# Attention and two feed-forward blocks on one core: w3 kept in DRAM as float32, and low parts of weights and of g made by VectorE

## Chip, core and metric

One core of a Trainium2 chip runs the whole program in one launch. The metric is device time in microseconds (us) of one execution; lower is better.

## What is computed

```python
# q, k, v: (4, 8, 576, 64), s: (4, 8, 576)
scores = q @ k.T / sqrt(64);  cum = cumsum(max(s, 0))
scores = where(causal, -1e9, scores + min(cum_k - cum_q, 0))
x = softmax(scores) @ v            # 32 heads, joined to (2304 tokens, 512)
h = x @ w_in                       # (512, 2048)
x = (h - tanh(h)) @ w_out          # g = h - tanh(h); (2048, 512)
y = ((x @ w1) * (x @ w2)) @ w3 @ w_out2    # (512, 1024) twice, (1024, 1024), (1024, 512)
```

The weights arrive as 64-bit floats, q, k, v and s as float32. The result must have float32 precision.

## The kernel before

**Precision.** TensorE multiplies in a rounded float32 format (`F32R`). An operand is therefore held as two tiles, a high part (the value rounded by a copy) and a low part (value minus high part), and a product is three matmuls: high x high, high x low, low x high (`mm3`, L113). `split` (L63) makes the two parts: the high part with a copy on ScalarE, the low part with a subtraction on GpSimd, unless the caller passes other engines as `hi` and `lo`. `plain` (L84) turns 64-bit weights into float32 with three integer operations on VectorE into a tile `cvt`; `convert` (L97) is `plain` followed by `split`.

**Stage 1, to about 430 us: attention and the first half of the first feed-forward block.** The 32 heads go in 16 pairs, each pair in two parts, along a list of numbered steps (L501 to L640): scores on TensorE, minimum and maximum on VectorE (L247), exponentials on ScalarE (L273), transposes and products with v on TensorE. Bias tiles come from GpSimd (L206, L218) and ScalarE (L208), out of a tile `cb` that a DMA spreads from DRAM. In between, `ffn` (L400) runs hidden chunks 0 to 7 of the 16 chunks of `w_in` and `w_out`, for nine blocks of 256 tokens: `h`, then tanh on ScalarE, `th = h - tanh(h)` on VectorE (L463), then g's high part `gh` and low part `gl` (L464 to L467), then `y` (L431). For blocks 0 and 1 `gh` is a ScalarE copy and `gl` a GpSimd subtraction; from block 2 both are VectorE's. `conversions` (L369) converts the 16 weight tiles of chunks 0 to 7; `parked` (L383) converts the 16 of chunks 8 to 15 and stores both parts to `wf_d` (`park`, L103), to be fetched when the first ones are free. Both use `split`'s GpSimd subtraction.

**Stage 2, about 430 to 622 us: chunks 8 to 15** for five blocks of up to 512 tokens (`ffn_rest`, L704). One step of `preparations` (L656) runs per chunk: it reads w1 and w2, forms sums for a seven-product matrix scheme and stores their two parts in `wg_d`; converts `w_out2` into the tiles `wo2`; and converts w3 in 8 pieces of two halves (L676 to L688). Pieces 6 and 7 stay in SBUF (`kept`), the others go to `w3_d` as two parts, 1,024 KB each.

**Stage 3, about 622 to 672 us: the product of w3 and w_out2** (`w3o`, L835 to L850), in eight groups of 24 matmuls in the order 6, 7, 4, 5, 0, 1, 2, 3. `fetch_w3` (L828) loads a piece from `w3_d` into one of two buffers `w3b`; the first two are the kept ones, so the load of a piece waits until the group two places earlier has been multiplied. ScalarE copies each result out (L844); `operands` (L759) and `weights` (L807) prepare the next stage on ScalarE and VectorE.

**Stage 4, to the end:** both products of x with w1 and w2, their elementwise product, and the product with the folded weights (L861 to L941), with weight tiles S and A loaded from `wg_d` (L787, L789).

**What sets the order.** TensorE's order is the order in which the program is written. For the other engines and for SP, whose queue issues the DMAs, a scheduler with a timeline of its own sets the order when the program is built; after that each engine works strictly in its order. Buffers are counted by pool tag: two of `raw` and two of `cvt` in pool `cv`, two of `park` in `wt`, one of `park` in `f2`, three each of `gh` and `gl`.

Of the kernel before, what the change touches and what calls it, by code (L numbers as in the profile page):

```python
# [37 lines left out]
def tile_kernel(ctx: ExitStack, tc: tile.TileContext, qk, v, s, w_in, w_out, w1, w2, w3t, w_o2, outT):  # L38
# [13 lines left out]

    cum_d = dr.tile([NH, S], F32, tag="cum_d", name="cum_d")
    yp_d = dr.tile([P, NC, NT], F32, tag="yp_d", name="yp_d")
    w3_d = dr.tile([NG, P, 2, 2, DM], F32, tag="w3_d", name="w3_d")
    wf_d = dr.tile([2 * (NF - F1), P, 2, DM], F32, tag="wf_d", name="wf_d")
    wg_d = dr.tile([NG, P, 7, 2, 2 * P], F32, tag="wg_d", name="wg_d")
    wo_d = dr.tile([7, 2, P, 2, 2, 2 * P], F32, tag="wo_d", name="wo_d")
# [4 lines left out]
    def split(dst_hi, dst_lo, src, hi=None, lo=None):  # L63
        i = (hi or nc.scalar.copy)(dst_hi, src)  # L64
        (lo or nc.gpsimd.tensor_sub)(dst_lo, src, dst_hi.bitcast(F32))  # L65
        return i
# [17 lines left out]
    def plain(raw, name, behind=None):  # L84

        r3 = raw.rearrange("p (f two) -> p f two", two=2)
        t = cv.tile([P, DM], U32, tag="cvt", name=f"cvt_{name}")
        i = nc.vector.tensor_scalar(out=t, in0=r3[:, :, 1], scalar1=3, scalar2=0x3FFFFFFF,
                                    op0=ALU.logical_shift_left, op1=ALU.bitwise_and)
        in_turn(i, behind)  # L90
        nc.vector.scalar_tensor_tensor(out=t, in0=r3[:, :, 0], scalar=29, in1=t,
                                       op0=ALU.logical_shift_right, op1=ALU.bitwise_or)
        nc.vector.scalar_tensor_tensor(out=t, in0=r3[:, :, 1], scalar=0xC0000000, in1=t,
                                       op0=ALU.bitwise_and, op1=ALU.bitwise_or)
        return t.bitcast(F32)

    def convert(raw, name, w=None, lo=None, behind=None):  # L97
        t = plain(raw, name, behind)
        w = slot(name) if w is None else w
        split(w[:, 0, :], w[:, 1, :], t, lo=lo)  # L100
        return w

    def park(raw, name, dst, pool, behind):  # L103

        w = convert(raw, name, pool.tile([P, 2, DM], F32R, tag="park", name=f"park_{name}", bufs=1), behind=behind)
        nc.sync.dma_start(dst, w.bitcast(F32))

    def fetch(name, src):
# [14 lines left out]
    with ExitStack() as actx:  # L123
# [245 lines left out]
        def conversions(fs):  # L369
            todo = [(d, f, src[f], f"{n}{f}") for f in fs for d, src, n in ((win, w_in, "win"), (wout, w_out, "wout"))]  # L370
            raws = []
            for m in range(2):
                raws.append(load_raw(*todo[m][2:], behind=latest[0]))
                yield
            for m, (d, f, src, n) in enumerate(todo):
                d[f] = convert(raws.pop(0), n, behind=least[0])
                if m + 2 < len(todo):
                    raws.append(load_raw(*todo[m + 2][2:], behind=latest[0]))
                yield
# [20 lines left out]
        def ffn():  # L400
            pend = []
            cut = {}

            def ready(blk):
                return blk < NB and all(written[b] >= min(S, (blk + 1) * BLK - S * b) for b in range(B))

            def cut_x(blk, lo):
                xs = cut.setdefault(blk, [])
                c, c0 = len(xs), blk * BLK
                x = f2.tile([P, 2, BLK], F32R, tag="xhl", name=f"xhl{blk}_{c}", bufs=6)  # L410
                split(x[:, 0, :], x[:, 1, :], xy[:, c, c0:c0 + BLK], lo=lo)
                xs.append(x)

            for blk in range(NB):
                c0 = blk * BLK
                while not ready(blk):
                    yield False
                while len(cut.get(blk, ())) < NC:
                    cut_x(blk, nc.vector.tensor_sub)
                xs = cut[blk]  # L420
                ys = []

                def add_y(f, gh, gl, end, ys=ys, blk=blk):
                    while f not in wout:
                        next(conv)
                    if f == 0:
                        ys.extend(ps_y.tile([P, 2, BLK], F32, tag=f"y{z}", name=f"y{z}_{blk}") for z in range(2))
                    for n, (z, x) in enumerate(((0, gh), (1, gh), (0, gl))):
                        for c in range(NC):
                            o = ys[c // 2][:, c % 2, :]  # L430
                            nc.tensor.matmul(o, wout[f][:, z, P * c:P * c + P], x,  # L431
                                             start=f == 0 and n == 0 and c % 2 == 0, stop=f == F1 - 1 and n == 2,
                                             skip_group_check=True)
                            if n == 1 and c == 1:
                                yield True
                    if f == F1 - 1:
                        after[1].append(end)

                def end_y(ys=ys, blk=blk, c0=c0):
                    for z in range(2):  # L440
                        yo = f2.tile([P, 2, BLK], F32R, tag="xhl", name=f"yo{z}_{blk}", bufs=6).bitcast(F32)
                        nc.scalar.copy(yo, ys[z])
                        nc.sync.dma_start(yp_d[:, 2 * z:2 * z + 2, c0:c0 + BLK], yo)

                for f in range(F1):
                    while f not in win:
                        next(conv)
                    late = written[B - 1] == S
                    ph = ps_a.tile([P, 512], F32, tag="s", name=f"h{blk}_{f}") if late else ps_h.tile([P, 512], F32, tag="h", name=f"h{blk}_{f}")
                    hh = ph[:, :BLK]  # L450
                    for c in range(NC):
                        pace[0] = mm3(hh, win[f], P * c, xs[c][:, 0, :], xs[c][:, 1, :], c == 0, c == NC - 1)
                        if c == 1:
                            yield True
                    t = f2.tile([P, BLK], F32, tag="th", name=f"th{blk}_{f}")
                    gh = f2.tile([P, BLK], F32R, tag="gh", name=f"gh{blk}_{f}", bufs=3)
                    gl = f2.tile([P, BLK], F32R, tag="gl", name=f"gl{blk}_{f}", bufs=3)

                    def tanh(t=t, hh=hh):
                        nc.scalar.activation(t, hh, AF.Tanh)  # L460

                    def rest(t=t, hh=hh, gh=gh, gl=gl, blk=blk):
                        nc.vector.tensor_sub(t, hh, t)  # L463
                        if blk < 2:  # L464
                            split(gh, gl, t)
                        else:
                            split(gh, gl, t, hi=nc.vector.tensor_copy, lo=nc.vector.tensor_sub)  # L467

                    after[0].append(tanh)
                    after[1].append(rest)  # L470
                    yield True
                    if len(pend) > late:
                        yield from pend.pop(0)
                    pend.append(add_y(f, gh, gl, end_y))
                    if f >= 3 and ready(blk + 1) and len(cut.get(blk + 1, ())) < NC:
                        cut_x(blk + 1, nc.vector.tensor_sub)
                    if blk == NB - 1 and f:
                        next(conv2, None)
                        next(conv2, None)
                    yield True  # L480
            for p in pend:
                yield from p
            yield True
            yield True
# [166 lines left out]
    def load_w3(f, z):  # L651
        return load_raw(w3t[f, :, 4 * z:4 * z + 4].rearrange("p m c -> p (m c)"), f"w3_{f}_{z}", behind=pace[0])
# [3 lines left out]
    def preparations():  # L656
# [19 lines left out]
        for f in range(NG):  # L676
            if f == NG // 2:
                for m in range(NG):
                    convert(load_raw(w_o2[m], f"wo2_{m}", behind=pace[0]), f"wo2_{m}", wo2[m], lo=nc.vector.tensor_sub)
                    yield  # L680
            pk = wt.tile([P, 2, 2, DM], F32R, tag="park", name=f"w3p{f}", bufs=2)
            for z in range(2):
                convert(load_w3(f, z), f"w3_{f}_{z}", pk[:, z], lo=nc.vector.tensor_sub)
                yield
            if f in W3ORDER[:2]:
                kept[f] = pk
            else:
                nc.sync.dma_start(w3_d[f], pk.bitcast(F32))  # L688

    with ExitStack() as bctx:  # L690
        b2 = bctx.enter_context(tc.tile_pool(name="b2", bufs=2, reuse_waits="tile"))
# [135 lines left out]

    def fetch_w3(f):  # L828
        if f not in w3b:
            w3b[f] = wt.tile([P, 2, 2, DM], F32R, tag="park", name=f"w3b{f}", bufs=2)  # L830
            nc.sync.dma_start(w3b[f].bitcast(F32), w3_d[f])
        return w3b[f]

    ctx.enter_context(tc.manual_schedule(engines={mybir.EngineType.PE}))
# [221 lines left out]
```

## Time and profile before

| what | value |
|---|---|
| median of 3 runs | 943.5 us (942.43 to 948.34) |
| the profiled execution: time, span | 942.7 us, 940.9 us |
| TensorE busy | 914.4 us, 97% of the span |
| VectorE, ScalarE, GpSimd busy | 641.4, 452.6, 211.7 us |
| mean granted TensorE clock | 0.995 |
| HBM read, written | 151.86 MB, 46.29 MB |

The span is the time from the first to the last instruction; 1.8 us of the execution lie around it. TensorE's busy time is modelled from pipelined matmuls, so gaps in it are the surer reading. Each engine works through its queue in order, so an instruction that waits holds up all that stand behind it.

### The profile page before, as it was taken

How to read it: one execution, taken by the hardware profiler on the slowest of the kernel's cores; microseconds unless marked ns; L12 is line 12 of the kernel's file. 1: busy time of each engine (PE TensorE's matmuls, PEld its weight loads, DVE VectorE, ACT ScalarE, POOL GpSimd, SP SyncE). 2: the span in 40 equal slices, each digit the busy share in tenths (PEclk: the TensorE clock that was granted, in tenths of full speed). 3: DMA queues.
4: the chain of work that ended last, by engine and by line, in shares of the span. 5: the costliest groups of instructions: out<-in, count | busy, mean ns of one | idle time of the engine just before them, and what ended most of it. 6: DMA issues, size and time to landing. Idle time of an engine off the chain costs nothing.

```text
span 940.9 us, 16373 instructions
## 1 busy us (share of the span) xinstructions
PE 914.4 (97%) x6022; PEld 800.3 (85%) x6025; DVE 641.4 (68%) x1403; ACT 452.6 (48%) x1061; POOL 211.7 (22%) x210
## 2 busy tenths in 40 slices
PE   8889999899999999999999999998999999999998
PEld 4567777788888889998888888987899999999998
DVE  7677777787777866776999978763145747564555
ACT  4567887777776753323434433342123432433133
POOL 2245856666555410000000000000011111111100
PEclk9799999999999999999999999999999999999999
DMA  5655365535454423489687736258399877777774
GB/s 161 196 164 170 114 205 182 168 137 179 154 169 147 152 98 100 169 308 405 250 293 279 265 110 209 85 207 291 119 319 325 322 257 271 262 271 258 284 267 148
DMA packets 59072, 199.21 MB, mean 212 GB/s; under 512 B 6544, under 2 KB 21040, under 8 KB 53360
## 3 DMA queue, kind: packets, MB, share of 16 engines
q1 hardware_dynamic: 58992, 198.17, 60.8%
q8 instruction: 47, 0.77, 0.3%
q14 instruction: 33, 0.27, 0.1%
HBM read 151.86 MB, written 46.29 MB: 211 GB/s over the span
## 4 chain that ended last, share of the span: by engine, by line
PE 81%; DMA 7%; DVE 5%; ACT 3%; issue 2%; POOL 1%; SPq 1%; ACTq 0%; DVEq 0%; POOLq 0%
PE hb L117 10%; PE yb L117 10%; PE h L117 9%; PE W L861 9%; PE y L431 9%; PE oW L924 5%; PE Y L861 5%; PE s_B L229 4%; PE pv L327 4%; PE oY L924 4%; PE pt_B L301 3%; PE w3o L117 2%; DMA w3b<-w_d 2%; PE V L861 2%; DMA cb<-cum_d 2%
## 5 line engine op out<-in xcount | busy, mean ns | idle before, releaser
L117 PE MATMUL h<-xhl,win 128*128 128x256 f32 x864 | 120.6, 286 | 2.8 <-DVE xhl L65 1.9
L117 PEld LDWEIGHTS h<-xhl,win 128*128 128x128 f32 x864 | 105.8, 188 | 13.4 <-issue 4.3
L994 POOL TENSOR_TENSOR xy<-c,c 128x384 f32<-128x384 f32 x12 | 15.4, 1280 | 425.4 <-DVE c L983 425.4
L117 PE MATMUL hb<-x,win 128*128 128x512 f32 (+1 forms) x480 | 104.9, 367 | 0.0
L117 PEld LDWEIGHTS hb<-x,win 128*128 128x128 f32 x480 | 83.9, 188 | 15.0
L206 POOL TENSOR_SCALAR pr<-cb,cq 128x384 f32<-128x384 f32 (+1 forms) x48 | 90.8, 1904 | 22.8 <-DMA cb<-cum_d 14.3
L117 PE MATMUL yb<-ghb,wout 128*128 128x512 f32 (+1 forms) x320 | 95.6, 367 | 0.0
L431 PE MATMUL y<-gh,wout 128*128 128x256 f32 x576 | 85.2, 287 | 0.5 <-DVE gh L64 0.5
L290 ACT ACTIVATE pr<-pr,nm 128x128 f32<-128x128 f32 (+2 forms) x120 | 71.5, 598 | 19.0 <-DVE nm L268 18.9
L431 PEld LDWEIGHTS y<-gh,wout 128*128 128x128 f32 x576 | 72.5, 189 | 3.7 <-issue 2.0
L117 PEld LDWEIGHTS yb<-ghb,wout 128*128 128x128 f32 x320 | 58.2, 188 | 9.9
L117 PE MATMUL yb<-glb,wout 128*128 128x512 f32 (+1 forms) x160 | 58.4, 367 | 0.0
L301 PE MATMUL pt_B<-ident,pr 96*128 96x96 f32 (+1 forms) x384 | 51.4, 256 | 1.4 <-DVE cq L601 0.9
L268 DVE CUSTOM_DVE_ANT_0 pr<-s_B,pr 96x512 f32<-96x512 f32 (+1 forms) x72 | 44.1, 638 | 8.7 <-PE s_B L229 8.7
L431 PE MATMUL y<-gl,wout 128*128 128x256 f32 x288 | 45.1, 279 | 3.2 <-POOL gl L65 2.7
L301 PEld LDWEIGHTS pt_B<-ident,pr 96*128 96x128 f32 (+1 forms) x384 | 41.2, 143 | 5.7 <-issue 3.3
L463 DVE TENSOR_TENSOR th<-h,th 128x256 f32<-128x256 f32 x72 | 30.0, 417 | 22.3 <-ACT th L460 21.6
L310 ACT COPY pf_B<-pt_B 128x512 f32<-128x512 f32 (+2 forms) x72 | 35.8, 499 | 19.3 <-PE pt_B L301 19.3
L460 ACT ACTIVATE th<-h 128x256 f32<-128x256 f32 x72 | 26.8, 373 | 34.4 <-PE h L117 34.3
L872 ACT COPY s<-Y 128x384 f32<-128x384 f32 x24 | 11.6, 482 | 63.0 <-PE Y L861 60.5
L431 PEld LDWEIGHTS y<-gl,wout 128*128 128x128 f32 x288 | 38.3, 188 | 3.8 <-POOL gl L65 3.1
L64 ACT CAST ghb<-thb 128x512 fp32r<-128x512 f32 (+1 forms) x40 | 23.2, 579 | 35.2 <-DVE thb L725 34.5
(215 smaller groups left out, 2076.7 us busy)
## 6 DMA issues: line engine op xcount, KB each, us to landing
S<-wg_d SPq DMA_DIRECT2D x24, 1024.0 KB
wo<-wo_d SPq DMA_DIRECT2D x42, 512.0 KB
A<-wg_d SPq DMA_DIRECT2D x24, 768.0 KB
qk<-in_qk SPq DMA_DIRECT2D x16, 576.0 KB
raw_win<-in_w_in SPq DMA_DIRECT2D x16, 512.0 KB
raw_wout<-in_w_out SPq DMA_DIRECT2D x16, 512.0 KB
raw_w<-in_w SPq DMA_DIRECT2D x16, 512.0 KB
wg_d<-pks SPq DMA_DIRECT2D x8, 1024.0 KB
```

The source lines that it names most:

```text
L117: i = nc.tensor.matmul(ps, a, b, start=first and n == 0, stop=last and n == 2, skip_group_check=skip)
L206: nc.gpsimd.tensor_scalar(out=t[:pw, e, :w], in0=p.cb[:pw, e, :w], scalar1=c, scalar2=0.0, op0=ALU.add, op1=ALU.min)
L229: latest[0] = nc.tensor.matmul(ps[e][:PW[i], o:o + k1 - k0], w[r, 0, CH0[i]:CH0[i] + PW[i]], x[r, 1, k0:k1], start=z == 0 and (not p.first ...
L268: least[0] = nc.vector.tensor_tensor_reduce(out=t[:pw, k0:k1], in0=ps[:pw, o:o + k1 - k0], in1=t[:pw, k0:k1], scale=-0.125, scalar=nm[:pw, ...
L290: last_exp[0] = nc.scalar.activation(t[:pw, :], t[:pw, :], AF.Exp, bias=m, scale=-1.0, accum_out=p.sums[:pw, e, c:c + 1])
L301: nc.tensor.transpose(pt[:, at:at + pw], p.pr[i][:pw, e, KC0[kj]:KC0[kj] + P], ident[:pw, :pw])
L310: (nc.vector.tensor_copy if j == "B2" and not p.first else nc.scalar.copy)(pf[:, :at], pt[:, :at])
L327: nc.tensor.matmul(p.pv[D * e:D * e + D, c:p.nq], p.vs[:, e, kj], pf[:, beg:end], start=z == 0, stop=z == len(todo) - 1, skip_group_check= ...
L431: nc.tensor.matmul(o, wout[f][:, z, P * c:P * c + P], x, start=f == 0 and n == 0 and c % 2 == 0, stop=f == F1 - 1 and n == 2, skip_group_c ...
L463: nc.vector.tensor_sub(t, hh, t)
L861: i = nc.tensor.matmul(ps[:, :T], w[:, x, P * j:P * j + P], b[:, y, j], start=first and j == n == 0, stop=stop and j == 1 and n == 2, skip ...
L924: nc.tensor.matmul(ps[:, :T], w[:, a, q % 2, P * j:P * j + P], x[:, b, q], start=o in ("B11", "B21", "T1") and q == z == 0, stop=o in ("T4 ...
```

## The change

There are four edits. (1) w3: pieces 0 to 5 are stored in `w3_d` as plain float32, one half at a time straight from the `cvt` tile, 256 KB per store instead of one store of 1,024 KB per piece; `fetch_w3` loads 512 KB into a `raw` buffer and makes the two parts there, the high part on ScalarE, the low part on VectorE. (2) `conversions`: the low part of the 16 weight tiles by VectorE instead of GpSimd. (3) `park`: the same for the 16 parked tiles. (4) block 1 of the first half of the feed-forward block: both parts of g by VectorE.

```diff
-    w3_d = dr.tile([NG, P, 2, 2, DM], F32, tag="w3_d", name="w3_d")
+    w3_d = dr.tile([NG, P, 2, DM], F32, tag="w3_d", name="w3_d")
...
     def park(raw, name, dst, pool, behind):
-        w = convert(raw, name, pool.tile([P, 2, DM], F32R, tag="park", name=f"park_{name}", bufs=1), behind=behind)
+        w = convert(raw, name, pool.tile([P, 2, DM], F32R, tag="park", name=f"park_{name}", bufs=1), lo=nc.vector.tensor_sub, behind=behind)
...
-                d[f] = convert(raws.pop(0), n, behind=least[0])
+                d[f] = convert(raws.pop(0), n, lo=nc.vector.tensor_sub, behind=least[0])
...
-                        if blk < 2:
+                        if blk < 1:
                             split(gh, gl, t)
                         else:
                             split(gh, gl, t, hi=nc.vector.tensor_copy, lo=nc.vector.tensor_sub)
...
-            pk = wt.tile([P, 2, 2, DM], F32R, tag="park", name=f"w3p{f}", bufs=2)
+            if f in W3ORDER[:2]:
+                kept[f] = wt.tile([P, 2, 2, DM], F32R, tag="park", name=f"w3p{f}", bufs=2)
             for z in range(2):
-                convert(load_w3(f, z), f"w3_{f}_{z}", pk[:, z], lo=nc.vector.tensor_sub)
+                if f in kept:
+                    convert(load_w3(f, z), f"w3_{f}_{z}", kept[f][:, z], lo=nc.vector.tensor_sub)
+                else:
+                    nc.sync.dma_start(w3_d[f, :, z], plain(load_w3(f, z), f"w3_{f}_{z}"))
                 yield
-            if f in W3ORDER[:2]:
-                kept[f] = pk
-            else:
-                nc.sync.dma_start(w3_d[f], pk.bitcast(F32))
...
     def fetch_w3(f):
         if f not in w3b:
+            raw = cv.tile([P, 2 * DM], U32, tag="raw", name=f"raw_w3b{f}").bitcast(F32).rearrange("p (z c) -> p z c", z=2)
+            nc.sync.dma_start(raw, w3_d[f])
             w3b[f] = wt.tile([P, 2, 2, DM], F32R, tag="park", name=f"w3b{f}", bufs=2)
-            nc.sync.dma_start(w3b[f].bitcast(F32), w3_d[f])
+            split(w3b[f][:, :, 0], w3b[f][:, :, 1], raw, lo=nc.vector.tensor_sub)
         return w3b[f]
```

TensorE's order stays as it was. The first place is SP's queue between stages 2 and 3, before the change (S and A are stage 4's weight tiles, w3b a piece of w3, yp the stored partial y):

```order
L709 DMA yp2048_7774<-yp_d_74 128x4x256
L787 DMA S_0_8166<-wg_d_77 128x2048
L789 DMA A_0_8168<-wg_d_77 128x1536
L787 DMA S_1_8243<-wg_d_77 128x2048
L789 DMA A_1_8245<-wg_d_77 128x1536
L831 DMA w3b4_8133<-w3_d_75 128x2048
L831 DMA w3b5_8164<-w3_d_75 128x2048
L831 DMA w3b0_8201<-w3_d_75 128x2048
```

And the same place after it:

```order
L831 DMA raw_w3b4_8109<-w3_d_75 128x1024
L709 DMA yp2048_7750<-yp_d_74 128x4x256
L831 DMA raw_w3b5_8143<-w3_d_75 128x1024
L787 DMA S_0_8148<-wg_d_77 128x2048
L789 DMA A_0_8150<-wg_d_77 128x1536
L787 DMA S_1_8231<-wg_d_77 128x2048
L789 DMA A_1_8233<-wg_d_77 128x1536
L831 DMA raw_w3b0_8183<-w3_d_75 128x1024
L831 DMA raw_w3b1_8226<-w3_d_75 128x1024
```

The loads of pieces 4 and 5 now stand ahead of the four loads of S and A, and move half the bytes.

The second place is VectorE's queue in stage 3, before the change (T, B and their `hl` tiles are operands of stage 4, wf a result of stage 3):

```order
L65 TENSOR_TENSOR B22hl_0_8238<-xy_71,B22hl_0_8238 128x768
L65 TENSOR_TENSOR T3hl_0_8285<-T3_0_8283,T3hl_0_8285 128x768
L772 TENSOR_TENSOR T4_0_8326<-xy_71,T2_0_8196 128x768
L772 TENSOR_TENSOR T1_1_8849<-xy_71 128x768
L65 TENSOR_TENSOR T4hl_0_8328<-T4_0_8326,T4hl_0_8328 128x768
L65 TENSOR_TENSOR T1hl_1_8851<-T1_1_8849,T1hl_1_8851 128x768
L772 TENSOR_TENSOR T2_1_8925<-xy_71,T1_1_8849 128x768
```

And after it:

```order
L65 TENSOR_TENSOR B22hl_0_8223<-xy_71,B22hl_0_8223 128x768
L65 TENSOR_TENSOR T3hl_0_8273<-T3_0_8271,T3hl_0_8273 128x768
L65 TENSOR_TENSOR w3b4_8111<-raw_w3b4_8109,w3b4_8111 128x2x512
L772 TENSOR_TENSOR T4_0_8317<-xy_71,T2_0_8178 128x768
L772 TENSOR_TENSOR T1_1_8843<-xy_71 128x768
L65 TENSOR_TENSOR T4hl_0_8319<-T4_0_8317,T4hl_0_8319 128x768
L772 TENSOR_TENSOR T2_1_8919<-xy_71,T1_1_8843 128x768
L65 TENSOR_TENSOR w3b5_8145<-raw_w3b5_8143,w3b5_8145 128x2x512
```

The low part of piece 4 now stands right behind T3hl, that of piece 5 behind three more subtractions of operands.

The third place is VectorE's queue near 46 us, before the change (nm are maxima of scores, xhl the low part of x for the feed-forward block, cvt_wout2 and cvt_win3 weights on their way from 64 bits):

```order
L65 TENSOR_TENSOR xhl0_2_597<-xy_71,xhl0_2_597 128x256
L91 SCALAR_TENSOR_TENSOR cvt_wout2_564<-raw_wout2_468,cvt_wout2_564 128x512
L88 TENSOR_SCALAR cvt_win3_621<-raw_win3_529 128x512
L93 SCALAR_TENSOR_TENSOR cvt_wout2_564<-raw_wout2_468,cvt_wout2_564 128x512
L257 TENSOR_REDUCE nm5_550<-s5_B2_0_582 96x1
L91 SCALAR_TENSOR_TENSOR cvt_win3_621<-raw_win3_529,cvt_win3_621 128x512
L257 TENSOR_REDUCE nm5_550<-s5_B2_1_583 96x1
L65 TENSOR_TENSOR xhl0_3_600<-xy_71,xhl0_3_600 128x256
```

And after it:

```order
L65 TENSOR_TENSOR xhl0_2_597<-xy_71,xhl0_2_597 128x256
L65 TENSOR_TENSOR win2_526<-cvt_win2_522,win2_526 128x512
L91 SCALAR_TENSOR_TENSOR cvt_wout2_564<-raw_wout2_468,cvt_wout2_564 128x512
L88 TENSOR_SCALAR cvt_win3_621<-raw_win3_529 128x512
L257 TENSOR_REDUCE nm5_550<-s5_B2_0_582 96x1
L93 SCALAR_TENSOR_TENSOR cvt_wout2_564<-raw_wout2_468,cvt_wout2_564 128x512
L257 TENSOR_REDUCE nm5_550<-s5_B2_1_583 96x1
L91 SCALAR_TENSOR_TENSOR cvt_win3_621<-raw_win3_529,cvt_win3_621 128x512
L65 TENSOR_TENSOR xhl0_3_600<-xy_71,xhl0_3_600 128x256
L65 TENSOR_TENSOR wout2_568<-cvt_wout2_564,wout2_568 128x512
```

One subtraction of a weight's low part (win2) has come in ahead of xhl0_3, the next (wout2) behind it.

## Rows read from the trace of the kernel before

**Rows 1.** Page, part 1: busy us (share of the span) and instructions.

```profile
PE 914.4 (97%) x6022; PEld 800.3 (85%) x6025; DVE 641.4 (68%) x1403; ACT 452.6 (48%) x1061; POOL 211.7 (22%) x210
```

**Rows 2.** Stretches: length, then busy us of PE, PEld, DVE, ACT, POOL, PEclk, DMA.

```profile
0.00:130.00 130.00, 119.86 (x848) 83.66 (x851) 97.56 (x255) 83.97 (x247) 58.26 (x67) 0.96 0.54 168
130.00:200.00 70.00, 65.18 (x565) 53.16 (x561) 50.11 (x153) 55.15 (x155) 47.95 (x51) 1.00 0.51 171
200.00:430.00 230.00, 228.11 (x1973) 203.12 (x1970) 166.47 (x475) 131.17 (x346) 74.39 (x70) 1.00 0.49 169
430.00:622.00 192.00, 192.00 (x939) 162.76 (x938) 156.02 (x281) 76.59 (x135) 0.00 (x0) 1.00 0.62 219
```

**Rows 3.** Timeline of PE, 622 to 673 us: start, us, instruction, idle before.

```profile
622.35 11.04 PE L117 MATMUL w3o<-wo,w3p 128*128 128x512 f32 x48
633.82 11.14 PE L117 MATMUL w3o<-wo,w3b 128*128 128x512 f32 x48 [0.42 <-DMA w3b<-w_d]
646.50 11.12 PE L117 MATMUL w3o<-wo,w3b 128*128 128x512 f32 x48 [1.54 <-DMA w3b<-w_d]
660.48 5.72 PE L117 MATMUL w3o<-wo,w3b 128*128 128x512 f32 x24 [2.85 <-DMA w3b<-w_d]
666.55 5.72 PE L117 MATMUL w3o<-wo,w3b 128*128 128x512 f32 x24 [0.35 <-DMA w3b<-w_d]
672.11 1.20 PE L861 MATMUL Y<-T1hl,S 128*128 128x384 f32 x6
```

**Rows 4.** Chain that ended last, in order of time, near 628 us.

```profile
628.03 5.65 DMA w3b<-w_d
```

**Rows 5.** Groups by line and shape, ScalarE and VectorE: busy us, mean ns.

```profile
L64 ACT CAST pks<-cs 128x1024 fp32r<-128x1024 f32 x8 | 8.4, 1054 | 8.1 <-DVE cs L666 8.0
...
L65 DVE TENSOR_TENSOR w3p<-cvt_w,w3p 128x512 fp32r<-128x512 f32 x16 | 10.9, 686 | 2.5 <-ACT w3p L64 2.4
...
L65 DVE TENSOR_TENSOR pks<-cs,pks 128x1024 fp32r<-128x1024 f32 x8 | 9.8, 1219 | 1.2 <-ACT pks L64 1.2
```

**Rows 6.** Timeline of VectorE near 630 us.

```profile
630.33 0.95 DVE L65 TENSOR_TENSOR T3hl<-T,T3hl 128x768 fp32r<-128x768 f32 x1
```

**Rows 7.** Timelines of PE and of GpSimd, 135 to 176 us.

```profile
135.62 0.74 PE L431 MATMUL y<-gl,wout 128*128 128x256 f32 x4 [0.89 <-POOL gl L65]
175.44 0.74 PE L431 MATMUL y<-gl,wout 128*128 128x256 f32 x4 [1.82 <-POOL gl L65]
...
170.26 3.96 POOL L206 TENSOR_SCALAR pr<-cb,cq 96x512 f32<-96x512 f32 x2
174.50 0.88 POOL L65 TENSOR_TENSOR gl<-th,gh 128x256 fp32r<-128x256 f32 x1
```

**Rows 8.** Groups by line and shape, GpSimd and VectorE: busy us, mean ns.

```profile
L65 POOL TENSOR_TENSOR win<-cvt_win,win 128x512 fp32r<-128x512 f32 x8 | 10.9, 1363 | 38.1 <-ACT win L64 38.1
...
L65 DVE TENSOR_TENSOR gl<-th,gh 128x256 fp32r<-128x256 f32 x56 | 25.3, 454 | 2.3 <-DVE gh L64 0.5
L64 DVE CAST gh<-th 128x256 fp32r<-128x256 f32 x56 | 18.0, 322 | 2.2
```

**Rows 9.** GpSimd and VectorE near 59 us; VectorE groups, first 130 us and whole.

```profile
58.83 1.28 POOL L65 TENSOR_TENSOR wout<-cvt_wout,wout 128x512 fp32r<-128x512 f32 x1 [4.87 <-ACT wout L64]
...
58.84 1.29 DVE L261 TENSOR_SCALAR nm<-nm 96x2 f32<-96x2 f32 x1
...
L65 DVE TENSOR_TENSOR xhl<-xy,xhl 128x256 fp32r<-128x256 f32 x8 | 6.7, 835 | 1.0 <-ACT xhl L64 1.0
...
L65 DVE TENSOR_TENSOR glb<-thb,ghb 128x256 fp32r<-128x256 f32 x8 | 3.4, 422 | 2.8 <-ACT ghb L64 2.8
```

**Rows 10.** Stretches from 32 to 44.7 us, columns as in rows 2.

```profile
32.00:34.40 2.40, 0.00 (x0) 0.00 (x0) 2.40 (x5) 1.82 (x5) 1.04 (x1) 1.00 0.49 124
34.40:44.70 10.30, 10.28 (x38) 6.40 (x39) 6.75 (x18) 4.67 (x16) 2.55 (x3) 0.50 0.59 200
```

**Rows 11.** Chain that ended last, first 130 us, shares by line.

```profile
by line: PE s_B L229 12.0%; DMA cb<-cum_d 9.1%; DVE nm L257 7.3%; PE pv L327 7.0%; issue 6.2%; PE s_B L245 5.6%; DMA rd<-rt 4.7%; PE pt_B L301 4.6%; PE h L117 4.4%; PE spare L213 3.7%; DVE xhl L65 3.5%; ACT pr L287 3.0%; PE y L431 2.7%; DMA
```

## The prediction

> **What bounds the kernel now.** I read the busy times first, then the same by stretch, then TensorE's gaps and what ended them. TensorE is busy in 97% of the span [rows 1], so only its gaps can be won. By stretch [rows 2] they are 10.1 us in the first 130 us (130 less 119.9), 4.8 us from 130 to 200, 1.9 us from 200 to 430, and none from 430 to 622, where whatever VectorE or ScalarE is spared is worth nothing. Stage 3 is read from TensorE's timeline instead [rows 3]: its first matmul starts at 622.35 and stage 4 at 672.11, 49.8 us for eight groups. A pair of groups without a gap takes 11.04 us, of which a tail of 0.16 overlaps what follows (666.55 + 5.72 = 672.27, while stage 4 starts at 672.11); less the tail and halved, a group is 5.44 us, and eight are 43.5 us. So 6.2 us of the stage are lost, and the four gaps named in the rows (0.42, 1.54, 2.85, 0.35, 5.2 us together) all end with a load of w3b. Elsewhere the one wait on an engine that the change touches is `y` waiting for GpSimd's `gl`, 0.89 and 1.82 us [rows 7].
>
> **Edit 1, w3.** In stage 2 ScalarE and VectorE lose work that hides behind a TensorE without gaps [rows 2], so nothing is won; `cvt` buffers are now held until their store has landed, 12 stores in all, at one conversion per chunk of some 5 us, which the same cover hides. In stage 3 the load of a piece waited for the group two places earlier, then took 5.65 us [rows 4], longer than the 5.44 us that the group in between covers, and its queue was shared with S and A. After the change that load goes into a `raw` buffer which is free long before (pieces 4 and 5 stand ahead of S and A in SP's queue), and what has to follow the group two places earlier is a ScalarE copy and a VectorE subtraction of 1,024 columns: 1.05 and 1.22 us for the same shape [rows 5], 2.3 us, with the handing over some 2.5 us. That fits into 5.44 us unless queues hold it. The tightest is piece 4: the group of piece 6 ends near 627.8 us (622.35 + 5.44), but VectorE has operands in front; T3hl, after which the subtraction now stands, ends at 631.28 [rows 6], so the subtraction ends near 632.5, and TensorE wants it at 633.2 (622.35 + 10.9). Piece 5 has three more subtractions in front, of 0.95 us as T3hl is [rows 6], from 632.5 to 635.4, a fourth ends near 636.3, and its own ends near 637.5 against 638.7. Pieces 0 to 3 have lighter queues. Later loads, half as long as before, are issued when a `raw` buffer is read out, some 6 us before their data are wanted (piece 4's is read out near 632.5, piece 0's data are wanted from 638.7 on). I take 5.9 of the 6.2 us, 0.3 being left for one late hand-over. Bounds: 6.2 us, and 0 if each of the six splits comes a microsecond late. What is late next is stage 4, whose order and loads move along unchanged.
>
> **Edit 4, g of block 1.** TensorE's two waits [rows 7] come from a `gl` that stood behind four bias operations; two of them alone ran from 170.26 to 174.2 and `gl` began at 174.50. On VectorE both parts take 0.32 + 0.45 us [rows 8], right behind `th`. Eight blocks' worth of chunks add 8 x 0.78 = 6.2 us to VectorE, beside TensorE. Of the 2.7 us I take 2.4; bounds 2.7 and 0.
>
> **Edits 2 and 3, low parts of weights.** 32 subtractions leave GpSimd (1.36 us each [rows 8]) and join VectorE at 0.69 us each, by the same shape [rows 5]. No TensorE wait is put down to GpSimd's weights, so nothing direct is won; what counts is that VectorE's maxima and low parts of x in the first 130 us now stand behind them. There are 17 in that stretch (16 of chunks 0 to 7 and the first parked one): 17 x 0.69 = 11.7 us, and VectorE goes from 97.6 to 109 of 130 us. Against that, VectorE is held up while GpSimd works: a 2-column operation beside a GpSimd subtraction of 1.28 us took 1.29 us, and the eight low parts of x took 0.835 us each where the same size takes 0.422 us late in the run [rows 9]; those eight alone are 3.3 us. Net 8.4 us more queue. Of the chain of the first 130 us, VectorE's two named lines hold 7.3 and 3.5% [rows 11], so 10.8% of 8.4 us, +0.9 us; I take +1.0. Bounds: +11.7 us, all of it on the path; and -1.2 us, if each removed subtraction had blocked VectorE for its whole length (17 x 1.36 = 23.1 us, less 11.7, times 10.8%). From 130 to 430 us another 15 parked subtractions (10.3 us) and the 6.2 us of edit 4 join a VectorE that is 72% busy in either stretch [rows 2]; TensorE's gaps there are short, and I take +0.1 us, bounds 0 and 16.5. SP's order moves a few stores of parked weights past loads of the next ones; each still waits for the same conversion, now without GpSimd's share.
>
> [...]
>
> **Sum.** -5.9 - 2.4 + 1.0 + 0.1 = -7.2 us. The profiled execution took 942.7 us, 1.8 us around a span of 940.9, and lies 0.8 us under the median of the three runs (943.5, 942.43 to 948.34). 942.7 - 7.2 = 935.5 us. A measurement of this kernel can tell about 1%, so faster means under 934.1 and slower over 952.9 us.
>
> **Rivals.**
>
> The splits come late. The loads' wait turns into a wait for ScalarE's and VectorE's queues. For it: piece 4 has only 0.7 us to spare, and ScalarE's results and high parts stand in one queue. Against it: from 635 us on those engines were mostly idle behind the same loads. Price: 5.9 us; 941.4 us.
>
> [...]
>
> The lock is returned in full. VectorE is relieved of all that GpSimd blocked, so the first 130 us lose 1.2 us instead of gaining 1.0, and the low parts of x, which end TensorE's waits there, come 0.41 us sooner each (0.835 less 0.422), three of the eight on the path by my estimate: 935.5 - 2.2 - 1.2 = 932.1 us. For it: the operation of 1.29 us [rows 9]. Against it: only 3.3 us of excess are plain in the means of xhl.
>
> VectorE becomes the bound of stage 1. It takes on 17 + 15 subtractions of 0.69 us and 6.2 us of g, 28.3 us in 430. From the point where 8.3 us of these (5.9 + 2.4) lie on the path the change gains nothing; at two thirds of them, 18.9 us, the time is 942.7 - 8.3 + 18.9 = 953.3 us. For it: strict order, and maxima that wait behind weights, as near 46 us, where one subtraction has moved ahead of xhl0_3. Against it: even with all of it VectorE is busy 84% in the first 130 us, (50.1 + 8.9) of 70 = 84% to 200, and under 80% after that.
>
> **How the numbers follow.** The sum as worked out: 50%, 932.5 to 939. Splits late: 15%. Clock dip gone: 17%. Lock returned: 12%. VectorE the bound: 6%. Faster by over 1% is a fifth of the first (10%), two thirds of the dip (11%) and three quarters of the lock (9%), 30%; slower by over 1% is the last, 6%; the rest, 64%, lies within 1%. The range holds the sum, the late splits and most of the dip and lock: 930.5 to 942 us. It leaves out the tail of VectorE as the bound and a dip and a lock together.
>
> **What would show it.** Right: starts of the groups of stage 3 every 5.44 us and no wait for w3b's load; no `y` waiting for `gl` between 130 and 180 us; stage 4 as long as before; gaps of the first 130 us between 9 and 13 us. Wrong: TensorE waits in stage 3 that end with ScalarE's or VectorE's part of w3b; a stage 1 in which TensorE waits for xhl, maxima or exponentials for 5 us more than before; a granted clock of 0.50 in another stretch than 34 to 45 us, or nowhere.

## The result, and the profile after

The changed kernel takes 931.5 us (median of 4; 930.46 to 934.4) where the kernel before takes 943.0 us (median of 4): a ratio of 0.9865, 95% interval 0.9824 to 0.9905. A second set of 4 gave 932.0 us and 0.9873 (0.9841 to 0.9904). Forecast were 935.5 us and a gain of 7.2; the gain is 11.5. The time lies inside the range, but the likeliest case, a change within 1% (64%), did not come: the kernel is 1.3% faster, which had 30%. The kernel before took 937 to 950 us over all its executions, so single profiles differ by some microseconds, and means are taken over as many executions as there were; two executions in a slow state, of 3,120 and 1,270 us, are left out of them.

Page, part 1, of the changed kernel, answering to [rows 1]:

```profile
PE 912.9 (98%) x6025; PEld 800.5 (86%) x6025; DVE 654.6 (70%) x1445; ACT 447.9 (48%) x1047; POOL 166.8 (18%) x170
```

The span fell by 11.1 us to 929.8, while VectorE's work rose by 13.2 us and GpSimd's fell by 44.9: more busy time on VectorE did not make the kernel slower. By stretch, columns as in [rows 2]:

```profile
0.00:130.00 130.00, 121.20 (x862) 84.56 (x864) 102.40 (x276) 84.71 (x249) 38.80 (x50) 0.95 0.53 171
130.00:200.00 70.00, 68.21 (x596) 56.48 (x593) 58.95 (x180) 54.98 (x152) 35.99 (x38) 1.00 0.54 182
200.00:430.00 230.00, 229.50 (x1962) 204.63 (x1961) 172.49 (x490) 131.73 (x345) 60.92 (x60) 1.00 0.51 176
430.00:616.90 186.90, 185.84 (x910) 157.07 (x909) 142.80 (x257) 65.28 (x117) 0.00 (x0) 1.00 0.59 200
```

TensorE's gaps are 8.8 us in the first 130 us (10.1 before), 1.8 to 200 (4.8), 0.5 to 430 (1.9), and 1.1 up to stage 3, where there were none. Timeline of PE in stage 3, answering to [rows 3]:

```profile
617.00 11.04 PE L117 MATMUL w3o<-wo,w3p 128*128 128x512 f32 x48
627.87 32.80 PE L117 MATMUL w3o<-wo,w3b 128*128 128x512 f32 x144
660.51 1.20 PE L863 MATMUL Y<-T1hl,S 128*128 128x384 f32 x6
```

All eight groups follow one another without a gap, 43.5 us from 617.00 to 660.51 where it was 49.8. The five largest waits of TensorE that are left (engine waited for, us in total, times, longest):

```profile
PE s_B L229 <- ACT rt L343: 3.3, 1, 3.3
PE spare L213 <- DVE identb L555: 2.0, 1, 2.0
PE h L117 <- DVE xhl L65: 2.0, 2, 1.1
PE s_B L229 <- ACT pr L286: 1.6, 2, 1.1
PE yb L117 <- ACT ghb L64: 0.8, 2, 0.5
```

The waits for w3b and for gl [rows 3, 7] are gone; new are those of yb for ghb, in stage 2. Gone too are these waits of the kernel before (pt are transposed probabilities, pf their copy for the product with v, cq the queries' part of the bias, th is h - tanh(h)):

```profile
PE pt_A L301 <- ACT pf_B L310: 1.6, 2, 0.9
PE s_B L229 <- ACT pf_B L310: 1.1, 2, 0.6
PE pt_B L301 <- DVE cq L601: 0.9, 1, 0.9
PE h L117 <- DVE th L463: 0.8, 1, 0.8
```

Read the same way from each timeline, the starts of the first `hb` (stage 2), of the first `w3o` (stage 3) and of the first matmul of stage 4 cut a profile into its stages; these are the eleven profiles of the kernels that separate the edits. "Low" lists the stretches at a granted clock of 0.50 from 50 us up to the end of stage 3 (start, length):

| kernel | stage 1 | stage 2 | stage 3 | stage 4 | low |
|---|---|---|---|---|---|
| before | 424.2 | 198.2 | 49.8 | 268.8 | none |
| before, again | 424.7 | 198.2 | 51.1 | 269.1 | 174.3 (3.4), 658.9 (6.8) |
| edit 1 | 421.5 | 198.2 | 43.5 | 269.2 | none |
| edit 4 | 421.1 | 198.2 | 52.4 | 269.8 | 138.9, 644.0, 664.5 (3.4 each) |
| edits 2, 3 | 421.0 | 198.2 | 48.9 | 269.4 | 58.5, 137.0 (3.4 each) |
| edits 2, 3, 4 | 417.3 | 198.2 | 52.5 | 270.0 | 641.1, 661.6 (3.4 each) |
| edits 1, 2 | 423.3 | 200.1 | 43.5 | 268.4 | 174.5 (6.8) |
| edits 1, 3 | 420.1 | 199.1 | 43.5 | 268.5 | none |
| edits 1, 2, 3 | 420.8 | 199.2 | 43.5 | 268.9 | 57.9, 136.4 (3.4 each) |
| after | 416.9 | 200.1 | 43.5 | 269.3 | none |
| after, again | 417.9 | 200.2 | 43.5 | 268.9 | none |

### The profile page after: what moved, and what is told of

Read it like the earlier page. It is cut to its first block, busy times and chain, and to the rows that moved or that the text cites. A ratio compares the mean times of both kernels' runs of the same rounds, so it can differ in the third digit from the quotient of the medians.

```text
span 929.8 us, 16349 instructions
## 1 busy us (share of the span) xinstructions
PE 912.9 (98%) x6025; PEld 800.5 (86%) x6025; DVE 654.6 (70%) x1445; ACT 447.9 (48%) x1047; POOL 166.8 (18%) x170
## 4 chain that ended last, share of the span: by engine, by line
PE 82%; DMA 7%; DVE 5%; ACT 4%; issue 1%; SPq 0%; POOL 0%; DVEq 0%; ACTq 0%
PE h L117 10%; PE y L431 9%; PE W L863 9%; PE hb L117 9%; PE yb L117 9%; PE oW L926 5%; PE Y L863 5%; PE w3o L117 5%; PE pv L327 4%; PE s_B L229 4%; PE oY L926 4%; PE pt_B L301 3%; PE V L863 2%; DMA raw_w<-in_w3t 2%; DMA rb<-rd 1%
## 5 line engine op out<-in xcount | busy, mean ns | idle before, releaser
L218 POOL TENSOR_SCALAR_AFFINE_SELECT pr<-pr 128x256 f32<-128x256 f32 (+2 forms) x60 | 29.4, 510 | 95.7 <-issue 95.2
L431 PE MATMUL y<-gl,wout 128*128 128x256 f32 x288 | 44.9, 279 | 0.0
L724 ACT ACTIVATE thb<-hb 128x512 f32<-128x512 f32 (+1 forms) x40 | 22.1, 553 | 42.7 <-PE hb L117 41.8
```

Source lines behind the costliest of these rows:

```text
L218: nc.gpsimd.affine_select(out=dg, in_=dg, pattern=[[0, 2], [-1, w - c]], compare_op=ALU.is_ge, fill=-8e9, base=0, channel_multiplier=1)
L431: nc.tensor.matmul(o, wout[f][:, z, P * c:P * c + P], x, start=f == 0 and n == 0 and c % 2 == 0, stop=f == F1 - 1 and n == 2, skip_group_c ...
```

## The experiments

**One part at a time.** Theories when these ran: P, the gain beyond the sum comes from VectorE no longer held up by GpSimd; S, it comes from ScalarE's lighter queue; against both, the prediction's sum. Each kernel is the one before with the named edits of the diff alone. Edit 1:

> The kernel before with edit 1 alone (w3 as float32). All theories: stage 3 shrinks from 49.8 to about 43.5 us and nothing else moves by more than a microsecond; about 6 us faster than before (some 937 us where before is 943). If stage 2 pays for the held cvt buffers (the comparison of the two profiles shows 1.9 us lost between 430 us and the start of stage 3, of which 1.06 us are waits for ghb and glb near 590 us), the same 1 to 2 us are lost here too and the gain is 4 to 5 us.

Edit 4:

> The kernel before with edit 4 alone (g of block 1 by VectorE). The prediction's sum: 2.4 us faster, the two waits of y for gl gone and all others as before. Theory P (the gain beyond the sum comes from VectorE no longer held up by GpSimd): about 2.5 to 3.5 us faster, since eight GpSimd subtractions of 0.9 us go. Theory S (it comes from ScalarE, which loses eight copies of gh as well, so that the waits of pt_A for pf_B, 1.6 us, go too): 4 to 5 us faster.

Edits 2 and 3:

> The kernel before with edits 2 and 3 alone (low parts of 32 weight tiles by VectorE). The prediction's sum: 1 us slower than before. Theory P: 2 to 4 us faster; in the first 130 us the low part xhl takes below 0.55 us instead of 0.835 us, the integer operations on weights 0.69 instead of up to 0.825 us. Theory S: within 1 us of before.

Edits 2 to 4:

> The changed kernel without edit 1 (edits 2 to 4 alone). The prediction's sum: 1.3 us faster than before. From the comparison of the profiles, in which stage 3 begins 7.3 us sooner until stage 2 gives 1.9 us back: 7 us faster if the loss of stage 2 belongs to edit 1, 5.4 us if it belongs to edits 2 to 4.

Later came the changed kernel and the kernel before once more, edits 1 and 2, edits 1 and 3, and the change without edit 4:

> The changed kernel once more, to have its spread beside the three kernels that follow, and a second profile of it. Both theories: 930 to 934 us. If the 1.9 us lost in stage 2 of its first profile are its own, stage 3 begins within 0.5 us of 617.0 us again; if they were chance (late loads of w3), it begins near 615 us.

> The kernel before once more, for a second profile. If the waits that the sum left out (pt_A for pf_B near 147 and 166 us, th near 349 us, gh and gl near 278 us) belong to every execution, they stand here again and stage 1 takes 423 to 425 us; if they were chance, most are gone and stage 1 takes about 421 us as in the kernel with edit 1 alone. A wait for w3b in stage 3 may again be followed by 3.4 us at a granted clock of 0.50.

> Edits 1 and 2 alone (w3, and low parts of the 16 tiles of chunks 0 to 7 by VectorE). If the gain of edits 2 and 3, 3 to 4 us, lies in the first 130 us, where VectorE is busiest: 3 us faster than edit 1 alone (some 934 us). If it lies in the parked tiles from 130 us on: as edit 1 alone (some 937 us), and stage 3 begins near 619 us.

> Edits 1 and 3 alone (w3, and low parts of the 16 parked tiles by VectorE). The mirror of the kernel with edits 1 and 2: if the gain lies from 130 us on, some 934 us, and the waits of pt_A for pf_B near 147 and 166 us, of th near 349 us are gone; if in the first 130 us, some 937 us.

> The changed kernel without edit 4 (g of block 1 by ScalarE and GpSimd again). If the edits add up: 1.5 to 2.5 us slower than the changed kernel (934 us), with two waits of y for gl near 135 and 173 us. If edit 4 is worth more once the rest is there, because its waits also bring stretches at the low clock: 935 to 937 us.

Measured (mean with its standard error, us; the ratio is to the kernel before measured beside it; the 92 leave out the first 4, with which the mean is the same):

| kernel | n | median | mean | ratio, 95% interval |
|---|---|---|---|---|
| before, all together | 92 | 943.9 | 943.5 ± 0.3 | |
| before, again (10 of the 92) | 10 | 944.3 | 942.6 ± 1.0 | 0.9992, 0.9964 to 1.0020 |
| edit 1 | 7 | 937.0 | 937.4 ± 1.3 | 0.9938, 0.9907 to 0.9969 |
| edit 4 | 10 | 941.5 | 941.0 ± 0.8 | 0.9975, 0.9952 to 0.9997 |
| edits 2, 3 | 10 | 939.3 | 939.6 ± 1.0 | 0.9953, 0.9926 to 0.9980 |
| edits 2, 3, 4 | 5 | 937.3 | 937.3 ± 0.9 | 0.9931, 0.9905 to 0.9957 |
| edits 1, 2 | 6 | 937.5 | 937.3 ± 0.5 | 0.9936, 0.9907 to 0.9965 |
| edits 1, 3 | 4 | 935.5 | 935.5 ± 1.0 | 0.9910, 0.9876 to 0.9945 |
| edits 1, 2, 3 | 4 | 932.0 | 932.4 ± 0.6 | 0.9886, 0.9856 to 0.9915 |
| after, both sets | 8 | 931.7 | 932.0 ± 0.5 | 0.9865 and 0.9873 |

Each edit can be read from three pairs of means. Edit 1: -6.1 (alone), -5.3 (on top of 2 to 4), -7.1 (on top of 2 and 3), mean -6.2. Edit 4: -2.5, -2.3, -0.5, mean -1.8. Edits 2 and 3 together: -4.0, -3.7, -5.0, mean -4.2. They add to -12.2 where the means of before and after differ by 11.5. So edits 1 and 4 came out near their prices, and edits 2 and 3 gained 4.2 us where 1.0 us of loss was forecast (1.1 with the stretch up to 430 us). S finds no support in the means: edit 4 alone brings 2.5 us (error 0.8), not 4 to 5, although the waits of pt_A for pf_B are gone from its profile, as S said. On top of edit 1, the second edit gains 0.2 us and the third 1.9, with errors of 1.3 and 1.6; as the last of the three, the third gains 4.8 (0.8) and the second 3.1 (1.2). So edit 3 carries a good part of the gain, and the share of edit 2 is not settled.

The profiles show why edit 2 is hard to read. TensorE's gaps in the first 130 us are 9.6 to 10.6 us in the six profiles without it and 7.1 to 9.6 in the fourteen with it. But the low stretch after 33 us lasts 10.2 us in all of the six, while nine of the fourteen, the changed kernel's two among them, have 3.4 us more at a granted clock of 0.50 before 66 us, one has 10 us more, and four have as much or less. Half of 3.4 us, 1.7, is my estimate of what that costs where TensorE is busy; it takes back the 1.6 us by which the mean gap fell.

Of the other expectations, stage 2 of edit 1 alone lost nothing (198.2 us). Edits 2 and 3 alone gained 4.0 us, with xhl at 483 ns, as P said; without edit 1 the kernel is 6.2 us faster than before, between the 5.4 and 7 put there. Edits 1 and 2 took as long as edit 1, which was to mean that the gain lies from 130 us on; edits 1 and 3, at 935.5, lie between the 934 and 937 put for the two cases. The second profile of the changed kernel has 200.2 us of stage 2 again, so that loss is its own, though stage 3 begins at 618.07 and not within 0.5 us of 617.0. The second profile of the kernel before has a stage 1 as long as the first, but only one of its two waits of pt_A for pf_B and a low stretch at 174.3 us: such waits come and go. Without edit 4 the kernel is only 0.5 us slower (error 0.8), although its two waits of y for gl stand there (3.6 us), so the 1.5 to 2.5 expected were missed.

**Is it GpSimd's work that cost?** To the changed kernel, idle subtractions on GpSimd are added; no weight waits for them:

```diff
+    def echoed(w):
+        nc.gpsimd.tensor_sub(echo, w[:, 0, :].bitcast(F32), w[:, 0, :].bitcast(F32))
+        return w
...
-                d[f] = convert(raws.pop(0), n, lo=nc.vector.tensor_sub, behind=least[0])
+                d[f] = echoed(convert(raws.pop(0), n, lo=nc.vector.tensor_sub, behind=least[0]))
```

and the same in `park`, for all but the last parked tile; `echo` is the last 512 columns of `xy`, written for good only later.

> The changed kernel, and beside it GpSimd again does a subtraction of 128x512 for 31 of the 32 weight tiles (high part minus itself, written to a region of xy that is overwritten later); no weight waits for it. [...] Theory C (what costs is that weights, their buffers and so the loads waited for GpSimd): within 1 us of the changed kernel. By the prediction's own figures (10.8% of the hold-up): 0.4 us slower.

The first 130 us of it by stretch; then its low parts of x there by line and shape (busy us, mean ns), and the same group of the changed kernel:

```profile
0.00:130.00 130.00, 121.15 (x851) 84.75 (x851) 105.32 (x276) 85.21 (x249) 60.72 (x67) 0.95 0.54 171
```

```profile
L65 DVE TENSOR_TENSOR xhl<-xy,xhl 128x256 fp32r<-128x256 f32 x9 | 5.5, 613 | 0.9 <-ACT xhl L64 0.7
```

```profile
L65 DVE TENSOR_TENSOR xhl<-xy,xhl 128x256 fp32r<-128x256 f32 x9 | 4.3, 476 | 1.5 <-ACT xhl L64 1.4
```

GpSimd is as busy as before the change (60.7 us; 58.3 in [rows 2]), but VectorE is held up again only in part: 613 ns, against 476 without these subtractions and 835 before [rows 9]. The time is 932.6 us. The second run stood beside the kernels of the next paragraph:

> The kernel with idle GpSimd subtractions once more, now beside the same kernel whose stores wait for them. Both theories: 931 to 933 us.

It took 934.5 us. Both together, 9 executions, have a mean of 933.5 ± 0.6: 1.6 us above the changed kernel, with an interval of 0.1 to 3.1. For this kernel theory P had put 3 to 5 us more than the changed kernel, and xhl above 0.6 us. The mean lies below those 3 to 5 us and above C's 1; something near a third of the gain may be GpSimd's work. As the hold-up of xhl came back by 137 of 359 ns, this does not say what all of it cost in the kernel before.

**Is it the stores that waited for GpSimd?** The view of SP's waits of the kernel before, for the stores of parked weights (L106):

```profile
SPq L106 <- POOL park_win L65: 29.3, 4, 8.8
SPq L106 <- POOL pr L218: 19.2, 5, 6.2
SPq L106 <- POOL park_wout L65: 15.9, 4, 8.4
```

SP's queue stood 64.4 us at these stores until GpSimd was done. After the change they wait for VectorE instead, 38.6 us in all, most of it in two lines:

```profile
SPq L106 <- DVE park_wout L65: 18.5, 5, 6.6
SPq L106 <- DVE gl L65: 15.3, 2, 8.2
```

SP did not wait less in sum: its waits of every kind are 47.5 us from 130 to 200 us and 175.2 from 200 to 430 before, 48.8 and 176.8 after. So 64.4 us is no price; what can count is which load stands behind a late store. Timeline of SP near 135 us, before and after:

```profile
132.01 0.52 SPq L70 DMA_DIRECT2D raw_win<-in_w_in  x1
137.50 0.33 SPq L106 DMA_DIRECT2D wf_d<-park_wout  x1
138.68 0.33 SPq L173 DMA_DIRECT2D qk<-in_qk  x1
```

```profile
133.27 0.33 SPq L106 DMA_DIRECT2D wf_d<-park_wout  x1
136.37 0.33 SPq L173 DMA_DIRECT2D qk<-in_qk  x1
```

The load of qk (q and k of the next heads) stands behind the store. What waits for it, ScalarE before and after, with TensorE's wait before:

```profile
143.64 1.15 ACT L178 CAST qkh<-qk 128x1152 fp32r<-128x1152 f32 x1 [1.92 <-DMA qk<-in_qk]
147.58 0.41 ACT L310 COPY pf_B<-pt_B 128x320 f32<-128x320 f32 x1
147.58 0.55 PE L301 MATMUL pt_A<-ident,pr 128*128 128x128 f32 x3 [0.87 <-ACT pf_B L310]
```

```profile
140.08 1.16 ACT L178 CAST qkh<-qk 128x1152 fp32r<-128x1152 f32 x1 [0.37 <-DMA qk<-in_qk]
143.34 0.41 ACT L310 COPY pf_B<-pt_B 128x320 f32<-128x320 f32 x1
```

TensorE was 1.1 us ahead at 132 us (`pt_B` from 133.13 to 132.01) and ScalarE's second copy of pf_B came 4.2 us sooner. From this comes theory Q: a store that waits for GpSimd holds up SP's queue, the loads behind it come late, and that costs. Test: in the kernel with idle subtractions, the parked store alone is made to wait for them.

```diff
-        nc.sync.dma_start(dst, w.bitcast(F32))
+        after_pe(nc.sync.dma_start(dst, w.bitcast(F32)), echoes[-1])
```

> The kernel with the idle GpSimd subtractions, but now the store of each parked weight also waits for GpSimd's subtraction, as in the kernel before. Theory Q: 2 to 4 us slower than the same kernel without that wait (which took 932.6 us), SP waiting for GpSimd some 40 us or more again. If SP's hold-up costs nothing: within 1 us of it.

> The kernel whose parked stores wait for the idle GpSimd subtraction, in one call with the one whose stores don't wait. Theory Q (a store that waits for GpSimd holds up SP's queue, and that costs): 3 to 6 us slower than without the wait. If the 5 us seen between the two earlier calls were chance: within 1 us.

SP's waits for GpSimd come back in part (25.5 us of the 40 or more expected):

```profile
SPq L118 <- POOL pr L230: 15.4, 5, 7.1
SPq L118 <- POOL xy L109: 10.1, 5, 6.9
```

The first run took 937.6 us (11 executions), the second 935.2 (6) beside 934.5 without the wait. Together 936.6 ± 0.7, 3.0 us above the kernel without the wait, interval 1.2 to 4.9 (2.7 if each is taken against the kernel before measured beside it). Where the two stood side by side the difference is 1.0 us, with an error of 1.5, and alone shows nothing. The wait is also not all that differs: the program built with it puts the load of the next weight ahead of the parked store again in three places of SP's queue, as in the kernel before, and the runs do not separate that order from the wait. With two subtractions in a row per parked weight:

> The same with two idle GpSimd subtractions in a row per parked weight, the store waiting for the second, so that each store comes some 1.3 us later still. Theory Q: another 1 to 4 us slower than with one. If only the first wait matters, or none: the same within 1 us.

936.6 us, mean 935.8 ± 1.1: no further cost, a miss. SP's waits for GpSimd rose from 25.5 to 33.6 us, but all waits of these stores together fell from 56.9 to 42.4. The other way round, edit 1 alone with the parked stores in GpSimd's queue (`nc.gpsimd.dma_start` in `park`):

> Edit 1 alone, and the stores of the 16 parked weights issued from GpSimd's queue instead of SP's; GpSimd still makes their low parts. Theory Q (in the kernel before, SP's queue stood still behind these stores until GpSimd had made the low part, 64 us of waiting in its profile, and the loads of qk and cb behind them came late): 2.5 to 4 us faster than edit 1 alone (at equal clock), ScalarE's waits for qk fall from 12.6 us to below 9 us, and the waits of pt_A for pf_B near 147 and 166 us are gone, although no subtraction has moved. If instead the subtractions themselves or the weights' lateness cost: as edit 1 alone.

939.9 us, mean 940.2 ± 0.5, 2.8 us slower than edit 1 alone (0.2 to 5.4): a miss for Q as put. ScalarE's wait for qk did fall (12.1 to 7.9 us), but the one for cb rose (6.7 to 9.1), and each store now takes GpSimd's queue for 0.6 us behind its bias work (the store of one tile at 178.31 us, its subtraction at 173.60). Taking the stores off SP's queue while GpSimd stays in the chain was not enough.

**Further versions.** Block 0's g by VectorE as well (`blk < 0`), the changed kernel with the parked stores in GpSimd's queue, and both:

> The changed kernel with g of block 0 by VectorE as well. Eight more pairs of 0.32 + 0.45 us join VectorE in its busiest 130 us, and eight GpSimd subtractions of 1.02 us and eight ScalarE copies of 0.41 us leave. No wait of TensorE for gl of block 0 stands in the profile of the changed kernel: within 1 us of it by every theory but a full VectorE, which gives 2 us slower or more.

> The changed kernel with the stores of the parked weights issued from GpSimd's queue. Theory Q: SP still waits 18.5 and 15.3 us for VectorE ahead of these stores in the changed kernel; without that, up to 1 to 2 us faster than the changed kernel. If those waits hide behind others on SP: the same, 930 to 933 us.

> The changed kernel with both additions that came out a little below it, g of block 0 by VectorE and the parked stores in GpSimd's queue. If the two add up: about 929.5 us; if they were chance: 931 to 932 us. Slower than 933 us if VectorE becomes full.

They took 931.1 (0.9869, 0.9838 to 0.9900), 930.7 (0.9865, 0.9834 to 0.9896) and 933.9 us (0.9880, 0.9846 to 0.9915). None can be told from the changed kernel (by means 1.0 and 1.4 us faster, errors 0.8 and 0.7, and 0.7 slower, error 1.5); the two do not add up, so they may well be chance.

## Why the prediction was right or wrong

**Stage 3: right, down to the tightest split.** Forecast for pieces 4 and 5 were subtractions that end near 632.5 and 637.5, and a want at 633.2; stage 3 began 5.35 us sooner, so that these are 627.1, 632.1 and 627.9 from the new start. Timeline of VectorE:

```profile
625.85 1.22 DVE L65 TENSOR_TENSOR w3b<-raw_w3b,w3b 128x1024 fp32r<-128x1024 f32 x1
630.71 1.22 DVE L65 TENSOR_TENSOR w3b<-raw_w3b,w3b 128x1024 fp32r<-128x1024 f32 x1
```

They end at 627.07 and 631.93. The rival of late splits did not come. "I take 5.9 of the 6.2 us" was right in sum (6.2 measured) by two errors that cancel. The term left out the low clock that came with such waits: in the five profiles without edit 1 stage 3 took 48.9 to 52.5 us, mean 50.9, against 43.5 with it, so 7.4 us, and three of the five have 6.8 us at a granted clock of 0.50 there. That the sum held is luck. And "nothing is won" in stage 2 should have been a loss of 1.4 us: it took 198.2 us in all five profiles without edit 1, and 198.2 to 200.8, mean 199.6, in the fifteen with it. "Which the same cover hides", said of the held `cvt` buffers and their stores, is the step that failed there. No wait of VectorE for a `cvt` buffer shows; its waits for loads of w3 do, 5.9 us before and 14.5 after. In the changed kernel:

```profile
SPq L687 <- DVE cvt_w L93: 36.2, 11, 6.0
```

```profile
582.89 0.43 DVE L88 TENSOR_SCALAR cvt_w<-raw_w 128x512 uint32<-128x512 uint32 x1 [3.07 <-DMA raw_w<-in_w3t]
...
587.46 0.50 PE L117 MATMUL yb<-ghb,wout 128*128 128x512 f32 x1 [0.33 <-ACT ghb L64]
```

The new stores of w3 halves (L687) wait on SP for their conversion, a late load of w3 follows, and soon after TensorE waits for ghb. That the one causes the other is read from these rows, not tested, and the store's wait alone does not decide it: with edit 1 alone SP waits 35.0 us at L687, VectorE 12.6 us for loads of w3, and stage 2 lost nothing (198.2 us).

**Edit 4: right in mechanism.** Both waits for gl went; the forecast took 2.4 us, and the pairs show 0.5 to 2.5, mean 1.8. Some may go to the next in line, which the prediction did not name: in the changed kernel h waits 1.12 us for xhl at 174.27.

**Edits 2 and 3: the step that failed.** "+1.0" for the first 130 us and "+0.1" up to 430 should have been -4.2 together, by the mean of three pairs. Two things were wrong. The sum charged VectorE's queue by its share of a chain, 10.8% of the net microseconds; VectorE took on 4.8 us of busy time in that stretch and TensorE's gaps shrank by 1.3 (8.8 from 10.1 us). And the bounds of the second stretch were "0 and 16.5", with nothing below zero, though 4.0 us of gaps stood there beside those for gl (4.8 less 2.7, plus 1.9); of all 6.7 us of gaps from 130 to 430, those for gl included, 2.3 are left. The step that was put at nothing without a reason is "SP's order moves a few stores of parked weights past loads of the next ones; each still waits for the same conversion, now without GpSimd's share". Putting that wait back, and with it that order, cost 3.0 us (1.2 to 4.9), and putting part of GpSimd's work back beside VectorE cost 1.6 us (0.1 to 3.1). Together that is 4.6 us, near the 4.2 that edits 2 and 3 gained. This speaks for the step, but does not close the case: a longer wait for GpSimd cost nothing more, and stores off SP's queue gained nothing. Which load behind the stores carries it stays open too. The rows near 135 us show one path, but with edit 1 alone (66.0 us of waits for GpSimd at these stores) only one of the two waits of pt_A for pf_B stands, and with edit 4 alone (56.6 us) and edits 1 and 2 (68.0 us) none.

**The rivals.** "The lock is returned in full" came nearest in time (932.1), in part by luck: xhl did fall, to 476 ns, and in the first 130 us TensorE's waits for it fell from 1.9 us to 0.8, near what that rival put there. With GpSimd's work beside it they are 1.6 us again, and yet most of the gain stays, while the stores have no place in that rival. The low parts of x take 613 ns with GpSimd's subtractions beside them and 476 without; by what, and whether this alone sets the time here, the runs do not show. VectorE as the bound of stage 1 did not come. The clock dip of the first 45 us did not go; it is 13.7 us long instead of 10.2, so the gain was made in spite of it. What its going is worth, to which the forecast gave 17%, no run shows by itself; what the runs show is that of the ten executions of edits 2 and 3 alone one took 935.5 us at a mean granted clock of 1.000 and one 944.9 us at 0.983. Of the signs of being right, three held and one did not: the gaps of the first 130 us are 8.8 us, under the 9 to 13 named.

## To carry to other kernels

Here SP's queue, which issues the loads, stood 64.4 us at stores until GpSimd was done, and the load of qk behind one of them was issued at 138.68 us where it was issued at 136.37 after the change. So read that queue's waits by what ends them and ask which load is wanted next; their sum is no price, as here it stayed the same (175.2 and 176.8 us from 200 to 430) while the time fell. Work moved to a busier engine can still win, as here by 4.2 us, so a share of the critical path is no price for it either, and a bound should reach below zero wherever gaps stand. When a wait is put back as a test, compare the order of the queue too: the scheduler may have moved it. Where a kernel's time varies by 1%, one profile does not tell which short waits belong to it; repeat the profile of before as well.

## What was not expected of the hardware

Gaps of 2 to 4 us in TensorE's work cost more than themselves in some executions here. Stage 3 of the second profile of before, timeline of PE, then its stretches, columns as in [rows 2]:

```profile
660.53 11.81 PE L117 MATMUL w3o<-wo,w3b 128*128 128x512 f32 x40 [3.94 <-DMA w3b<-w_d]
```

```profile
650.00:658.90 8.90, 6.58 (x28) 4.83 (x27) 3.01 (x5) 2.94 (x5) 0.00 (x0) 1.00 0.95 328
658.90:665.70 6.80, 5.17 (x12) 4.14 (x13) 0.00 (x0) 0.00 (x0) 0.00 (x0) 0.50 0.77 321
665.70:674.00 8.30, 8.30 (x38) 6.78 (x37) 0.00 (x0) 0.59 (x1) 0.00 (x0) 1.00 0.00 2
```

TensorE stood 3.94 us for w3b, and the granted clock was 0.50 until 665.7. In the profile of edit 4 alone, and then in that of edits 2 and 3, a group of 24 matmuls of the same shape after a gap of 1.97 and of 1.99 us:

```profile
664.49 7.33 PE L117 MATMUL w3o<-wo,w3b 128*128 128x512 f32 x24 [1.97 <-DMA w3b<-w_d]
```

```profile
656.36 5.72 PE L117 MATMUL w3o<-wo,w3b 128*128 128x512 f32 x24 [1.99 <-DMA w3b<-w_d]
```

7.33 against 5.72 us: 1.6 us for one stretch of 3.4 at a granted clock of 0.50, after the one gap and not after the other. Stage 3 had such stretches in three of the five profiles with w3b waits and in none of the fifteen without. A wait of y for gl was followed by the same: 2.64 us, ended at 173.07 in the kernel with edits 1 and 2, then 6.8 us at 0.50 from 174.5.
